# Linear attention and a squared-ReLU MLP in one kernel: the second half's two output products as one product by seven, with its sums made by accumulating transfers

## The chip, the cores and the metric

The kernel runs on one core of a Trainium2 chip. The metric is the device time of one execution in microseconds (us); the kernel before takes 407.9 us as the median of three runs (407.67 to 407.97). Durations and waits below come from one profiled execution of it, whose span is 406.3 us.

## The reference

```python
x = A_x                                   # 2048 tokens x 512 channels, float32
xn = layernorm(x)
# attention: 32 heads of 16 channels, no softmax
q, k, v = split(xn @ wqkv)                # phi(t) = t + 1 if t > 0 else exp(t); + 1e-6
kv = phi(k)^T v;  z = sum over tokens of phi(k)        # for each head
o = phi(q) @ kv / (phi(q) . z + 1e-6)
# MLP on x with 1376 hidden channels
h = relu(xn @ w1 + b1) ** 2
out = x + o @ wo + h @ w2 + b2
```

`xn` feeds both branches. `B_x` is not used.

## The kernel before, in words

All matrix products are float32 by three passes: an operand is split into a high part (the value rounded to the type that TensorE takes, a copy on ScalarE) and the rest (a subtraction on VectorE, `rest_of`, line 125, or the second half of `split`, line 122), and `PASSES` multiplies high by high, high by rest and rest by high. So each 128x128 by 128x512 product is three "wide" matmuls of 512 columns. A matmul of 256 columns is called a half here.

**The first quarter** (lines 526 to 1000) goes over 16 tiles of 128 tokens: normalise, transpose, project the keys, and sum `kx`. From it `matrix()` makes `m`, 512x512, which holds kv and `wo` in one, so that the attention output is `queries @ m`, where `queries` are phi(q) divided by the denominator.

**The main part** runs over two pairs of blocks of 512 tokens (`for n in range(2)`, line 1060): blocks 3 and 2, then blocks 1 and 0. In each pair:

- The loop over `p` (line 1194) makes the queries and the hidden units of both blocks: seven passes (`order`: two of queries, five of hidden units). A pass is a 2x2 block product made with seven products in place of eight (sums and differences of blocks ahead, sums of results behind). Each of the seven (`product`, line 494) is six wide matmuls. The operands on the weight side (`aop`) are made from w1 and wqkv with `chunk_sums`, `chunk_split` and `last_split`, in both pairs anew; those on the token side are `T`.
- Between these products stand the products of block t1's hidden units with w2 (`mlp_2`, line 502): a unit chunk of 128 takes 12 wide matmuls for a block of 512 tokens, into four accumulators.
- After the loop come the attention product of block t1, then for block t2 the same `mlp_2` for one chunk after the other, and its attention product. The last 96 hidden channels are apart: `last_2` and, for 32-row quarters, `quarters_2`.
- The attention product is `add_attention` in the first pair. In the second pair it is a product by seven again, for each block apart: class `Seven` (lines 1000 to 1054), whose matmuls are halves (`run`, line 1046), whose results are added to the residual by VectorE (`into`, line 1054).
- `steps_of` (line 421) turns each chunk of raw queries into divided ones: `phi_T`, `weighted`, `sums`, `quotients`, `divide`.

The residual x is loaded into `res`, the bias b2 is added to it by GpSimd's accumulating transfers (`add_bias`, line 1166, issued at line 1170), the accumulator is added by VectorE (`add`, line 1178), and the rows are stored (line 1182). The order of the work is written out by hand: `AT`, `AE` and `TM` (lines 1068 to 1086) say how many of the small steps go at which place. `matrix_sums` (line 975) prepares the sums of `m`'s blocks through DRAM. Every engine runs its instructions in program order; SyncE (SP) and GpSimd (POOL) issue transfers in program order too.

Of the kernel before, what the change touches and what calls it, by code (L numbers as in the profile page):

```python
# [13 lines left out]
P = 128  # L14
H = 32
# [3 lines left out]
def kernel(  # L19
# [400 lines left out]

    def steps_of(t, j, done=False, parts=False):
# [8 lines left out]
        def weighted():  # L430
            pz = w512(f"pz{t}_{j}", "p", 6)
            tiles.append(pz)
            nc.scalar.activation(pz, o, AF.Identity, bias=zc[:, 1, j:j + 1], scale=zc[:, 0, j:j + 1])  # L433

        def sums():
            pt = w512(f"pt{t}_{j}", "p", 6)
            den = small.tile([P, H], F32, name=f"dt{t}_{j}", tag="den")
            nc.vector.transpose(blocks(pt), blocks(tiles[0]))
            nc.vector.tensor_reduce(den, heads_of(pt), axis=AX.X, op=OP.add)
            tiles.append(den)  # L440

        def quotients():
            pz, den = tiles
            nc.vector.tensor_scalar(den, den, 1e-6, None, op0=OP.add)
            nc.vector.reciprocal(den, den)
            nc.vector.transpose(by_heads(heads_of(pz)), by_heads(den[:, :, None].to_broadcast([P, H, D // H])))

        def divide():
            nc.vector.scalar_tensor_tensor(o, o, 1e-6, tiles[0], op0=OP.add, op1=OP.mult)

# [524 lines left out]
    def matrix_sums(stage):  # L975

        t = [two(f"mr{r}") for r in range(2)]
        for r in range(2):
            nc.gpsimd.dma_start(t[r], md[:, 2 * r:2 * r + 2])
# [7 lines left out]
        def high(x, h, to, at):  # L987
            copy("act", h.bitcast(F32R), x)
            nc.gpsimd.dma_start(mtd[0][:, to, at], h)

        def low(x, h, to, at):
            nc.vector.tensor_tensor(out=x.bitcast(F32R), in0=x, in1=h, op=OP.subtract)
            nc.gpsimd.dma_start(mtd[1][:, to, at], x)
# [6 lines left out]
    class Seven:  # L1000

        def __init__(self, t, pairs=range(2)):
            self.t = t
            self.at = [slice(r * BT // 2 + pairs[0] * P, r * BT // 2 + (pairs[-1] + 1) * P) for r in range(2)]
            self.o = [[q[t][:, 2 * c:2 * c + 2, at] for c in range(2)] for at in self.at]

        def sums_o(self):

            (a11, a12), (a21, a22) = self.o
            return [lambda: self.op(a22, a21, a22, OP.add), lambda: self.op(a21, a11, a21, OP.subtract),  # L1010
                    lambda: self.op(a11, a22, a11, OP.subtract), lambda: self.op(a12, a12, a11, OP.subtract)]

        def op(self, o, x, y, how):
            nc.vector.tensor_tensor(out=o, in0=x, in1=y, op=how)

        def load_m(self):

            self.mt = both("mt", ("xs0h", "xs0l"))
            for o, src in zip(self.mt, mtd):
                nc.gpsimd.dma_start(f32(o), src)  # L1020

        def parts(self, src, to, order):

            highs, lows = [], []
            for c, at in order:
                h, l, x = (a[:, 2 * c:2 * c + 2, at] for a in (*to, src))
                highs.append(lambda h=h, x=x: copy("act", h, x))
                lows.append(lambda h=h, l=l, x=x: rest_of(l, x, h))
            return highs, lows

        def parts_o(self):

            self.s = both(f"so{self.t}", ("xs1h", "xs1l"))
            one, two = self.at
            return self.parts(q[self.t], self.s, ((1, one), (0, one), (0, two), (1, two)))

        def run(self, ps, left, right, e, first=False):

            c, r = left[1:]
            for i in range(2):  # L1040
                for n, (u, v) in enumerate(PASSES):
                    at = slice(r * (BT // 2) + e * P, r * (BT // 2) + (e + 1) * P)
                    a = aT[self.t, 2 * c + i][:, u, at] if left[0] == "a" else self.s[u][:, 2 * c + i, at]
                    w, k, z = right
                    b = (m if w == "m" else self.mt)[v][:, 2 * k + i, z]
                    nc.tensor.matmul(ps, lhsT=a, rhs=b, start=first and i == 0 and n == 0, stop=False,  # L1046
                                     skip_group_check=True)

        def into(self, ps, k, a):

            r = res[self.t, k][:, a]
            if a != LO and a != HI:
                r, ps = r.rearrange("p (a z) -> p a z", a=2), ps[:, None, :].to_broadcast([P, 2, D // 2])
            nc.vector.tensor_tensor(out=r, in0=ps, in1=r, op=OP.add)

    ALL = slice(0, D)

    last = TB - 1
    res = {}
    for n in range(2):  # L1060
        t1, t2 = NB - 1 - 2 * n, NB - 2 - 2 * n
        x1, x2 = xsb
        tag = "acc" if n else "ps"

        order = [("q", 0), ("w", 0), ("q", 1), *(("w", k) for k in range(1, NP))]
        NO = len(order)

        AT = (((0, 0, 0, 0, 0, 0, 0, 0, 0),
# [14 lines left out]
               (0, 0, 0, 0, 0, 0, 0, 2, 0)))[n]  # L1083
        AE = ((3, 1, 2, 3, 5, 2, 0, 1, 4, 5, 2),
              (2, 3, 2, 2, 0, 0, 0, 0, 0, 0, 0))[n]
        TM = {(1, 0): 4, (1, 4): 2, (1, 6): 1, (2, 4): 2, (3, 7): 1, (3, 0): 1, (4, 7): 1} if n else {}

        def matrix_step(p, at):
            do(m_sums, TM.get((p, at), 0))

        steps = {t1: [], t2: []}
        r2 = [work.tile([P, k, 512], F32, name=f"r2{u}{n}", tag=f"r{u}") for u, k in zip("abc", (4, 4, 3))]
        waiting = [*range(NF - 2, -1, -1), NF - 1]
        r2 = {f: r2[k // 4][:, k % 4] for k, f in enumerate(waiting)}
        m_sums = matrix_sums([r2[f] for f in waiting[:4]]) if n else []

        def last_units(rz):
            nc.scalar.activation(rz, rz, AF.Square)
            sz, rests = hidden_last(f"sz{n}", rz)

            def packed():
                lqs.append(quarters(f"sz{n}", rz, sz[0], work, "heads"))

            return sz, rests, packed

        lqs = []

        if n == 0:

            more()  # L1110
            pz2 = bank("pz0b")
            plain_1(pz2, z, x2)
            more()

            rz = r2[1]
            relu(rz, pz, NF - 1)
            relu(r2[NF - 1], pz2, NF - 1)
            do(extra, 2)
            values()
            do(extra, len(extra))  # L1120
        else:
            w2next = []
            pz = bank(f"pz{n}", "acc")
            plain_1(pz, z, x1)
        q.update({t1: four(f"q{t1}", "r2"), t2: four(f"q{t2}", "r1")})
        attention_places("r3", "r0")
        w = load_1(*order[1])
        s = {}
        if n:
            rz = w512(f"rz{n}", "p", 6)  # L1130
            relu(rz, pz, NF - 1)
            sz, sz_rests, packed = last_units(rz)
            sz_rests()
            packed()

        w2order = [NF - 1, *range(NF - 1)]

        def next_2(t):

            do(w2next, 2 - highs.pop(0))  # L1140
            if t + 1 < NF and (n == 0 or t >= TB - 1):
                f = w2order[t + 1]
                w2next.extend(piece_2(f, place(f)))

        def high_2():
            do(w2next)
            highs[0] = 1

        highs = [0] * NF
        if n:  # L1150
            next_2(0)


        banks = [bank(f"b{n}_{k}") for k in range(4)]
        t5, biased = None, []

        def load_res(t):
            for k in range(2):
                r = two(f"res{t}_{k}")
                i = t * TB + 2 * k  # L1160
                nc.sync.dma_start(r, xf[i * P:(i + 2) * P, :].rearrange("(i p) d -> p i d", i=2))
                for i in range(2):
                    res[t, 2 * k + i] = r[:, i, :]
                biased.append(r)

        def add_bias():
# [428 lines left out]
```

## Time and profile before

| | |
|---|---|
| median of three runs | 407.9 us |
| span of the profiled execution | 406.3 us |
| TensorE (PE) busy | 401.3 us, 99% |
| VectorE (DVE) busy | 329.2 us, 81% |
| ScalarE (ACT) busy | 273.3 us, 67% |
| GpSimd (POOL) busy | 57.3 us, 14% |
| moved by transfers | 55.31 MB, 136 GB/s over the span |
| GpSimd's transfer queue q0 | 9.44 MB |

How to read the profile: "PE" is the matmuls, "PEld" the loads of their stationary operand, which overlap them. In rows of a group, "x16 | 10.5, 688" is the count, the busy us in all and the mean ns of one. Matmuls are pipelined, so the time that one costs is read from the distance of starts and not from its 390 ns. In the table of stretches, "DMA share" is the mean busy share of the core's 16 transfer engines and GB/s what they moved. A few per cent of the matmul records are missing, so counts of matmuls are worked out from the code.

### The profile page before, as it was taken

The numbers are of one execution on the slowest core, as the hardware profiler recorded it, in microseconds if no ns is written. First come the engines' busy times: TensorE is split into PE (matmuls) and PEld (weight loads), VectorE is DVE, ScalarE is ACT, GpSimd is POOL, SyncE is SP. The second block draws the span as 40 slices with busy tenths as digits, with TensorE's granted clock in tenths as the row PEclk, the third lists the DMA queues.
The fourth block names the chain that finished last, engine by engine and source line by source line (L and its number), as shares of the span: only waits on it lengthen the run. The fifth ranks groups of instructions, "written<-read, shape, count | busy, mean of one in ns | idle before, by whom it ended". The sixth has DMA issues, their size and how long they took to land.

```text
span 406.3 us, 5887 instructions
## 1 busy us (share of the span) xinstructions
PE 401.3 (99%) x2011; PEld 334.1 (82%) x2011; DVE 329.2 (81%) x603; ACT 273.3 (67%) x478; POOL 57.3 (14%) x93
## 2 busy tenths in 40 slices
PE   8999999999999999999999999999999999999996
PEld 7888888888788888888878888888888888888895
DVE  5886666497898999988349998598989688989983
ACT  5777777456788789887728751578678857957430
POOL 5444333220000000030000300102200013000300
PEclk9999999999999999999999999999999999999999
DMA  5857656820463231291563912824331739306512
GB/s 210 275 166 230 208 157 205 241 45 0 121 193 80 77 103 27 85 224 29 186 231 124 227 38 91 231 53 129 122 113 52 207 110 305 53 34 224 105 26 105
DMA packets 48623, 55.31 MB, mean 136 GB/s; under 512 B 8593, under 2 KB 31377, under 8 KB 48082
## 3 DMA queue, kind: packets, MB, share of 16 engines
q1 hardware_dynamic: 44994, 45.50, 36.4%
q0 software_dynamic: 3520, 9.44, 9.9%
q8 instruction: 16, 0.26, 0.3%
q14 instruction: 13, 0.11, 0.1%
q10 hardware_dynamic: 80, 0.00, 0.0%
HBM read 40.90 MB, written 12.85 MB: 132 GB/s over the span
## 4 chain that ended last, share of the span: by engine, by line
PE 97%; DMA 1%; DVE 1%; ACT 0%; issue 0%
PE b L498 33%; PE acc L133 32%; PE pk L378 11%; PE kx L398 11%; PE acc L1046 2%; PE acc L509 2%; PE pz L133 1%; PE x L1046 1%; PE xl L1046 1%; DMA x<-in_A_x_dram 1%; PE b L133 1%; PE pz0b L133 1%; PE pt L310 0%; PE yl L1046 0%; PE y L1046 0%; PE acc L516 0%
## 5 line engine op out<-in xcount | busy, mean ns | idle before, releaser
L133 PE MATMUL acc<-w2r,s 128*128 128x512 f32 x477 | 113.0, 390 | 0.0
L133 PEld LDWEIGHTS acc<-w2r,s 128*128 128x128 f32 x477 | 89.3, 188 | 19.0 <-issue 0.7
L498 PE MATMUL b<-T,aop 128*128 128x512 f32 x336 | 83.5, 390 | 0.0
L498 PEld LDWEIGHTS b<-T,aop 128*128 128x128 f32 x336 | 63.0, 188 | 13.9 <-ACT t L114 0.8
L398 PE MATMUL kx<-pk,tok 128*128 128x512 f32 x192 | 46.0, 390 | 0.0
L398 PEld LDWEIGHTS kx<-pk,tok 128*128 128x128 f32 x192 | 36.0, 188 | 7.6 <-ACT pk L114 0.2
L1170 POOL DMA_DIRECT2D res<-in_B_b_dram x16 | 14.4, 1038 | 173.6 <-DVE S L736 85.9
L498 PE MATMUL b<-xs0h,aop 128*128 128x512 f32 x112 | 36.9, 391 | 0.0
L114 ACT ACTIVATE aop<-S 128x512 fp32r<-128x512 f32 x28 | 17.5, 624 | 13.1 <-DVE S L736 13.1
L359 POOL TENSOR_TENSOR tok<-xp,tok 128x512 fp32r<-128x512 f32 x15 | 19.8, 1320 | 39.8 <-ACT tok L114 39.8
L498 PEld LDWEIGHTS b<-xs0h,aop 128*128 128x128 f32 x112 | 21.0, 188 | 4.4
L125 DVE TENSOR_TENSOR w2r<-r,w2r 128x512 fp32r<-128x512 f32 (+2 forms) x35 | 23.8, 683 | 0.7 <-ACT w2r L114 0.6
L114 ACT ACTIVATE w2r<-r 128x512 fp32r<-128x512 f32 x32 | 19.6, 618 | 6.1 <-PE acc L133 4.7
L122 DVE TENSOR_TENSOR aop<-S,aop 128x512 fp32r<-128x512 f32 x28 | 19.3, 689 | 4.5 <-ACT aop L114 4.1
L498 PE MATMUL b<-xs0l,aop 128*128 128x512 f32 x56 | 21.8, 389 | 0.0
L122 DVE TENSOR_TENSOR s<-c,s 128x512 fp32r<-128x512 f32 x20 | 13.6, 689 | 7.6 <-ACT s L114 7.4
L498 PE MATMUL b<-xs1h,aop 128*128 128x512 f32 x56 | 19.5, 389 | 0.0
L114 ACT ACTIVATE T<-Tf 128x512 fp32r<-128x512 f32 x16 | 9.5, 625 | 14.4 <-DVE Tf L679 14.3
L114 ACT ACTIVATE c<-b 128x512 f32<-128x512 f32 x28 | 16.4, 585 | 2.8 <-PE b L498 2.6
L433 ACT ACTIVATE pz<-q,zc 128x512 f32<-128x512 f32 x16 | 12.9, 808 | 6.3 <-DVE q L419 6.3
L1178 DVE TENSOR_TENSOR res<-acc,res 128x512 f32<-128x512 f32 x16 | 10.5, 688 | 7.9 <-PE acc L133 5.1
L369 ACT ACTIVATE k<-pk 128x512 f32<-128x512 f32 x16 | 9.5, 593 | 9.7 <-PE pk L378 9.5
(265 smaller groups left out, 853.8 us busy)
## 6 DMA issues: line engine op xcount, KB each, us to landing
r<-in_B_w_dram SPq DMA_DIRECT2D x49, 256.0 KB, 3.5
res<-in_A_x_dram SPq DMA_DIRECT2D x8, 512.0 KB, 4.7
res<-in_B_b_dram POOLq DMA_DIRECT2D x16, 256.0 KB, 5.8
out_dram<-res SPq DMA_DIRECT2D x15, 256.0 KB, 2.1
via<-xp SPq DMA_DIRECT2D x5, 512.0 KB, 2.6
xg<-via SPq DMA_DIRECT2D x20, 128.0 KB, 2.8
xTd<-t SPq DMA_DIRECT2D x8, 256.0 KB, 3.4
x<-in_A_x_dram SPq DMA_DIRECT2D x4, 512.0 KB, 4.4
```

The costliest lines, as they stand in the source:

```text
L114: nc.scalar.activation(o, i, AF.Copy, bias=bias)
L122: ENG[el].tensor_tensor(out=l, in0=src, in1=f32(h), op=OP.subtract)
L125: nc.vector.tensor_tensor(out=l, in0=src, in1=f32(h), op=OP.subtract)
L133: nc.tensor.matmul(ps, lhsT=a[u], rhs=b[v], start=first and n == 0, stop=last and n == 2)
L359: ENG[el].tensor_tensor(out=l, in0=src, in1=f32(h), op=OP.subtract)
L378: nc.tensor.matmul(ps, lhsT=cols(i)[u][:, j, slot(i)], rhs=w[v][:, j, :], start=first and n == 0, stop=last and n == len(steps) - 1)
L398: nc.tensor.matmul(kxp[c], lhsT=tok[i][:, u, c * P:(c + 1) * P], rhs=pk[i][:, v], start=i == 0 and (u, v) == first, stop=i == NT - 1 and ( ...
L433: nc.scalar.activation(pz, o, AF.Identity, bias=zc[:, 1, j:j + 1], scale=zc[:, 0, j:j + 1])
L498: nc.tensor.matmul(ps, lhsT=a[u][:, j * P:(j + 1) * P], rhs=b[v][:, j, :], start=first and j == 0 and n == 0, stop=last and j == 1 and n == 2,
L1046: nc.tensor.matmul(ps, lhsT=a, rhs=b, start=first and i == 0 and n == 0, stop=False, skip_group_check=True)
L1170: nc.gpsimd.dma_start(r[:, i], b2[None, :].partition_broadcast(P), accum_op=OP.add)
L1178: nc.vector.tensor_tensor(out=r[:, a:z], in0=ps, in1=r[:, a:z], op=OP.add)
```

## The change

The first pair is as it was, but for two things: after each product its weight-side operand is stored to DRAM (`keep_operands`), and the differences of w2's blocks are made once (`w2_sums`: 12 subtractions on VectorE, stored to `w2sd`). The second pair is written anew:

- **Loop.** The seven passes run back to back without `mlp_2`. Operands come from DRAM (`load_operand`, 256 KB each, two passes ahead) in place of being split again. Sums of results go two ways: ScalarE copies one bank into another (with the bias) and the next product accumulates on it, or VectorE adds. Hidden units are kept squared, as float32, for both blocks: `h[r, c, k]` with r the block and c the parity of the chunk.
- **One product by seven** then does w2 and attention together: left is [hidden, queries] of both blocks (2x2: block by parity half), right is [w2; m] (2x2: parity half by output half). Each of the seven products, in the order M4, M1, M2, M6, M5, M7, M3, has parts 0, 1, 2 (five chunks of hidden units) and "q" (two chunks of queries): 42 wide matmuls, but for M3. M4 and M1 begin inside the loop's last pass.
- **Left sums** (`sum_of`) are four, made in place: sum 1 = A21 + A22, sum 3 = A21 - A11, sum 2 = sum 1 - A11, sum 4 = A12 - sum 2 up to sign, with A11 and A12 negated by ScalarE (`negate`). Each is four accumulating transfers from SBUF to SBUF on GpSimd's queue: three of 512 KB and one of 256 KB. M6 needs sum 2, M5 sum 1, M7 sum 3, M3 sum 4. Before its product a part is split (`left`): ScalarE's copy, VectorE's subtraction.
- **Output transposed.** For all but M3 the weights stand on the stationary side, every second column of 256 (`columns`), and 512 tokens stream; the result has channels on partitions. VectorE transposes it by 32x32 blocks (`turned_out`), and it is added to a residual block (`into`), by accumulating transfers of 256 KB or by VectorE. The residual blocks are loaded and stored in pieces of 32x16x64 (256 bytes in a row; `load_block`, `store_block`), 64 KB each. M3 is not transposed: 84 halves, added to rows that went out to DRAM and came back.

```diff
+    def keep_operands(p, *which):
+        for s in which:
+            nc.sync.dma_start(aopd[p][s], f32(src...))
+    def load_operand(p, name):
...
+        nc.sync.dma_start(f32(o), aopd[p][s][...])
...
-    class Seven:
...
-                nc.tensor.matmul(ps, lhsT=a, rhs=b, start=first and i == 0 and n == 0, stop=False,
...
+    def sum_of(n, *which):
+        for part in which:
+            o, a = (source(rc, part) for rc in SUMS_OF[n])
+            nc.gpsimd.dma_start(o, a, accum_op=OP.add)
+    def mul(name, ps, *which, first=False):
+        for part in which:
+            for a, b in zip(half_units[name, part], rights(name, part)):
+                for e in range(2):
+                    for n, (u, v) in enumerate(PASSES):
+                        nc.tensor.matmul(ps[e], lhsT=columns(b[u], e, None), rhs=a[v],
+    def turned_out(name, ps, half=None):
...
+                nc.vector.transpose(t.rearrange("p (b c e) -> p e b c", e=2, c=Q)[:, e],
+                                    by_blocks(src[e])[:, 8 * u:8 * u + 8])
+    def into(r, half, tiles, eng="dma"):
...
+                nc.gpsimd.dma_start(o, tiles[u], accum_op=OP.add)
...
+    sum_of(1, 1, 2)
+    mul("M4", X, 1, 2)
+    sum_of(3, 0, 1, 2)
+    load_block(0, 0, res_1[:, 0])
+    load_block(1, 1, res_1[:, 1])
+    left("M4", "q")
+    negate(0, "q")
+    sum_of(2, 0, 1, 2)
+    sum_of(1, "q")
...
+    sum_of(3, "q")
+    load_right("M5")
+    m1 = turned_out("M1", Ac, 0)
+    sum_of(2, "q")
+    m4 = turned_out("M4", X, 0)
+    into(0, 0, m1)
+    into(1, 0, m4)
+    mul("M2", Bc, 0, 1, 2, "q", first=True)
+    sum_of(4, 0, 1, 2, "q")
+    left("M6", 0, 1, 2)
+    load_right("M7")
+    mul("M6", Ac, 0, 1, 2)
+    left("M5", 0)
+    left("M6", "q")
+    mul("M6", Ac, "q")
...
+    into(0, 0, m2)
+    store_block(0, 0)
...
+    load_block(0, 1, res01)
+    mul("M5", Ac, 0, 1, 2, "q")
+    load_right("M3")
+    left("M7", 0, 1, 2, "q")
+    m5 = turned_out("M5", Ac, 1)
+    into(0, 1, m5, "dve")
+    store_block(0, 1, rowsd)
+    mul("M7", Y, 0, 1, 2, "q", first=True)
+    left("M3", 0, 1, 2, "q")
...
```

The denominator's 1e-6 moves into `zc`, which saves `steps_of` one small VectorE instruction for each chunk.

GpSimd's queue at its end, before: the sums of `m`'s blocks and the bias rows (`res`) of the second pair.

```order
L993 DMA mtld_1070<-mr0_2498 128x2x256
L993 DMA mtld_1070<-mr1_2499 128x2x256 x2
L1020 DMA mth_3238<-mthd_1069 128x2048
L1020 DMA mtl_3239<-mtld_1070 128x2048
L1170 DMA res1_0_3075<-in_B_b2_dram 128x512 x2
L1170 DMA res1_1_3077<-in_B_b2_dram 128x512 x2
L1170 DMA res0_0_3613<-in_B_b2_dram 128x512 x2
L1170 DMA res0_1_3615<-in_B_b2_dram 128x512 x2
```

The same place now, from the second part of sum 1 to the residual sum of M2. `h11`, `h10`, `h00`, `h01` are the hidden blocks, `h114` and `h4` their fifth chunks, `q0` and `q1` the queries, `res1` and `res10` residual blocks; L1596 is `sum_of`, L1719 `into`.

```order
L1596 DMA h10_2667<-h00_2665 128x1024 x2
L1596 DMA h4_2669<-h4_2669 128x512
L1596 DMA h00_2665<-h11_2668 128x1024 x2
L1596 DMA h4_2669<-h114_3098 128x512
L1596 DMA q0_2573<-q0_2573 128x1024
L1596 DMA q0_2573<-q1_2572 128x1024
L1596 DMA q1_2572<-q0_2573 128x1024
L1719 DMA res1_3341<-M1t0_3422 128x512
L1719 DMA res1_3341<-M1t1_3425 128x512
L1719 DMA res10_3093<-M4t0_3436 128x512
L1719 DMA res10_3093<-M4t1_3439 128x512
L1596 DMA h01_2666<-h00_2665 128x1024 x2
```

What moved: the bias transfers are gone (the bias is added by ScalarE in `turned_out`), the transfers of `m`'s sums went to SP, and in their place GpSimd issues all left sums, with the residual sums of M1 and M4 ahead of sum 4 and those of M2 behind it.

ScalarE at the M6 product, now (before, this stretch held the squares and splits of one unit chunk after the other). `M6_0` to `M6_q` are the parts of M6's left side, `rightM5` and `w2r0` M5's right side.

```order
L114 ACTIVATE M6_2_3508<-h4_2669 128x512
L114 ACTIVATE rightM5_3511<-T1r0_3412 128x2x256
L114 ACTIVATE rightM5_3511<-T1r2_3414 128x2x256
L114 ACTIVATE w2r0_1020<-T1r4_3416 128x256
L114 ACTIVATE M5_0_3554<-h11_2668 128x1024
L114 ACTIVATE M6_q_3557<-q1_2572 128x1024
L114 ACTIVATE M5_1_3572<-h11_2668 128x1024
```

What this shows: M6's last part stands behind M5's right side and first part on ScalarE; it reads `q1`, which is the last transfer of sum 2.

SP at the end, before: the last residual rows, and the last stores.

```order
L1161 DMA res0_0_3613<-in_A_x_dram 128x2x512
L1161 DMA res0_1_3615<-in_A_x_dram 128x2x512
L213 DMA w2r0_1020<-w2r0_1020 64x512
L478 DMA s1_0_10_3789<-s1_0_10_3789 64x512
L1182 DMA out_0_dram<-res0_0_3613 128x512 x2
L1182 DMA out_0_dram<-res0_1_3615 128x512
```

SP at the end now: `T3r` is M7's right side, `b22r` that of M3, `res01` the residual block that M5 and M3 end in, `rowsd` its way through DRAM.

```order
L1619 DMA T3r4_3522<-w2sd_1099 128x256
L1695 DMA out_0_dram<-res1_3341 32x16x64 x4
L1691 DMA res01_3615<-in_A_x_dram 32x16x64 x4
L1619 DMA b22r0_3669<-in_B_w2_dram 128x2x256
L1619 DMA b22r2_3671<-in_B_w2_dram 128x2x256
L1619 DMA b22r4_3673<-in_B_w2_dram 128x256
L1695 DMA rowsd_3699<-res01_3615 32x16x64 x4
L1941 DMA rows_3767<-rowsd_3699 128x4x256
```

What moved: a store of finished output, which waits for M2's residual sum, now stands ahead of the last residual block and of the last operand loads; before, no operand load stood behind a store there.

More of the change, by code (lines that the diff above doesn't have):

```diff
@@ L978, in matrix_sums @@
         for r in range(2):
-            nc.gpsimd.dma_start(t[r], md[:, 2 * r:2 * r + 2])
+            nc.sync.dma_start(t[r], md[:, 2 * r:2 * r + 2])
         def op(o, x, y):
@@ L998, in matrix_sums @@
                                                               (low, 1), (low, 2), (low, 3)))]
-    class Seven:
[L1002 to L1054, printed above, removed]
@@ L1554 @@
[L1554 to L1566 removed]
+                next_2(fa + 1)
@@ new lines @@
+            product(C, S1, [T[1][:, u] for u in range(2)], True)
+            keep_operands(p, 2)
+            t5_ = w512(f"t5_{p}", "p", 6)
+            copy("act", t5_, C)
+            step(at_p[1])
+        else:
+            do(bias, 2)
+            mlp_2(acc, pa, s.pop(pa))
+        if was:
+            product(before, A22b, [T[4][:, u] for u in range(2)], False, True)
+            if was == "w":
+                c21 = w512(f"c21_{p}", "p", 6)
+                relu(c21, before, pb)
+            elif p == 1:
+                copy("dve", q[t1][:, pb], before)
+            else:
+                phi_T(q[t1][:, pb], before)
+                steps[t1] += steps_of(t1, pb, True, True)
@@ new lines, with second_sums @@
+        if kind == "w":
+            high_2()
+        if p == 0:
+            last_sums(4, difference_high, difference_low)
+        if kind == "w":
+            relu(r2[fa], c12, fa)
+        else:
+            steps[t2] += steps_of(t2, fa)
+        step(at_p[5])
+        if kind == "w" and fa:
+            next_2(fa + 2)
+        def second_sums(f=pb, first=not was):
+            if first:
+                for k in range(TB):
+                    last_2(acc[k], k, sz, True, False)
+            else:
+                mlp_2(acc, f, s.pop(f))
@@ new lines @@
+    for k in range(TB):
+        at = slice((2 + k % 2) * Q, (3 + k % 2) * Q)
+        nc.tensor.matmul(ends[k], lhsT=zq[0][at, k * P:(k + 1) * P], rhs=w2s["q"][at, HI], start=False, stop=False)
+    chunks = [(a, b) for part in (0, 1, 2, "q") for a, b in zip(half_units["M3", part], rights("M3", part))]
+    for k in range(TB):
+        for n, (a, b) in enumerate(chunks):
+            three(ends[k], [v[:, k * P:(k + 1) * P] for v in a], b, False, n == len(chunks) - 1)
+        nc.vector.tensor_tensor(out=rows[:, k], in0=ends[k], in1=rows[:, k], op=OP.add)
+        i = t1 * TB + k
+        nc.scalar.dma_start(of[i * P:(i + 1) * P, HI], rows[:, k])
```

1149 lines of the change are left out of this document (706 added, 443 removed), and 21 rows, old and new, of the table AT.

## The prediction

> **What bounds the kernel now.** First the page's busy times and slices:
>
> ```profile
> span 406.3 us, 5887 instructions
> PE 401.3 (99%) x2011; PEld 334.1 (82%) x2011; DVE 329.2 (81%) x603; ACT 273.3 (67%) x478; POOL 57.3 (14%) x93
> ...
> PE   8999999999999999999999999999999999999996
> PEclk9999999999999999999999999999999999999999
> DMA  5857656820463231291563912824331739306512
> ```
>
> TensorE is full in every slice between the first and the last, at full clock; the transfer engines are busy in bursts. The chain of waits says the same:
>
> ```profile
> PE 97%; DMA 1%; DVE 1%; ACT 0%; issue 0%
> ```
>
> So matmuls set the time, and I need the price of each kind. TensorE's timeline gives it, as the distance of starts:
>
> ```profile
> 363.23 22.04 PE L133 MATMUL acc<-w2r,s 128*128 128x512 f32 x96
> 385.10 0.28 PE L1046 MATMUL xl<-mh,aTsr 128*128 128x256 f32 x1
> ...
> 395.13 3.59 PE L133 MATMUL acc<-w2r,s 128*128 128x512 f32 x15
> ...
> 402.24 0.40 PE L509 MATMUL end<-w2r,s 128*128 128x256 f32 x2
> ```
>
> A wide matmul costs (385.10 - 363.23) / 96 = 0.228 us. Between 385.10 and 395.13 stand the 84 halves of one block's attention product: 10.03 / 84 = 0.119 us each, slightly over half a wide one. The last matmul starts at 402.24, 4.1 us before the end.
>
> What could become late is read from the table of stretches (columns: span, busy us and counts of PE, PEld, DVE, ACT, POOL, clock, DMA share, GB/s): the halves, the loop, the first pair's second part, the loop of the second pair.
>
> ```profile
> 385.10:395.10 10.00, 10.00 (x85) 10.00 (x84) 8.54 (x16) 4.55 (x9) 0.00 (x0) 1.00 0.12 26
> 120.00:160.00 40.00, 40.00 (x178) 33.14 (x177) 36.87 (x70) 33.52 (x60) 0.00 (x0) 1.00 0.28 77
> 200.00:240.00 40.00, 40.00 (x182) 32.60 (x182) 32.13 (x56) 26.07 (x44) 3.56 (x4) 1.00 0.63 187
> 280.00:320.00 40.00, 40.00 (x179) 33.12 (x178) 36.02 (x69) 31.25 (x58) 4.04 (x6) 1.00 0.41 122
> ```
>
> VectorE works up to 36.9 us of 40 and TensorE still doesn't wait; transfers have room.
>
> **Matmuls.** By the code, the second pair's w2 and attention take 251 wide matmuls, 178 halves and 8 quarters before. Now: six products of 42 wide are 252, with 12 for the last channels 264; M3's 84 halves and 8 more, and some ten small pieces. That is 13 x 0.228 = 3.0 us more and 86 x 0.119 = 10.3 us less: **-7.3 us**, and 400.6 us in place of 407.9 if nothing waits.
>
> **First pair.** Storing operands (28 of 256 KB) goes where the DMA share was 0.28. Making w2's differences adds 12 subtractions to VectorE:
>
> ```profile
> L122 DVE TENSOR_TENSOR aop<-S,aop 128x512 fp32r<-128x512 f32 x28 | 19.3, 689 | 4.5 <-ACT aop L114 4.1
> ```
>
> 12 x 0.69 = 8.3 us, beside the first pair's attention (48 wide, 10.9 us) and w2 products. In 200 to 240, VectorE has 7.9 us free. I take 0; without that cover it is the 8.3.
>
> **The loop without `mlp_2`.** Each pass is 42 wide matmuls, 9.57 us. The attention steps that lay beside twice the matmuls now stand close together:
>
> ```profile
> L446 DVE STREAM_TRANSPOSE pz<-dt 128x512 f32<-128x512 f32 x16 | 11.4, 712 | 0.6
> L438 DVE STREAM_TRANSPOSE pt<-pz 128x512 f32<-128x512 f32 x16 | 11.3, 704 | 0.0
> L439 DVE TENSOR_REDUCE dt<-pt 128x32 f32<-128x512 f32 x16 | 11.0, 686 | 0.6
> L445 DVE RECIPROCAL dt<-dt 128x32 f32<-128x32 f32 x16 | 5.7, 353 | 0.6
> ```
>
> With two 0.69 operations, one step costs VectorE 3.8 us; eight cost 31. Adds and squares of five unit passes, four each at 0.69, are 14; the adds of the two query passes 5.5; left parts of M4 and M1 8.7; right sides 3.5: about 63 of 67 us. In the windows above VectorE kept 92% with TensorE full; 94% is at the edge. Token-side sums lie ahead of the loop as before. I take 0, up to 3 as an upper end; a gain is excluded, as TensorE was full. Dropped splits of aop free VectorE and ScalarE only.
>
> **Weights by every second column.** No row loads weights with a step. Contiguous ones:
>
> ```profile
> L498 PEld LDWEIGHTS b<-T,aop 128*128 128x128 f32 x336 | 63.0, 188 | 13.9 <-ACT t L114 0.8
> ```
>
> 188 ns lie under the 228 of a wide matmul. Up to 228 ns a stepped load costs nothing; doubled (376) it would cost 0.15 x 252 = 37 us. I take 0, since there is no row to say that the step costs.
>
> **The accumulating transfers.** This decides. After's sums are 16 transfers (12 of 512 KB, 4 of 256 KB: 7.3 MB), the residual sums by transfer 12 of 256 KB (3.1 MB): 10.5 MB, nearly all within the last 80 us. The only accumulating transfers of before are the bias, four at a time:
>
> ```profile
> 175.76 2.90 POOL L1170 DMA_DIRECT2D res<-in_B_b_dram  x3 [85.94 <-DVE S L736]
> 180.58 0.89 POOL L1170 DMA_DIRECT2D res<-in_B_b_dram  x1 [1.91 <-issue]
> ```
>
> and all of them by their line:
>
> ```profile
> L1170 POOL DMA_DIRECT2D res<-in_B_b_dram x16: 853/990/1295, 175.8 to 381.1; - x16
> ...
> DMA to landing us min/median/max: 4.5/5.8/10.3
> ```
>
> GpSimd takes 1 us to issue one, and holds the fourth back. What the wires did meanwhile, beside plain loads elsewhere:
>
> ```profile
> 178.00:184.00 6.00, 6.00 (x28) 4.95 (x28) 4.75 (x9) 5.26 (x9) 1.56 (x2) 1.00 0.96 153
> 339.00:342.00 3.00, 3.00 (x15) 2.47 (x14) 1.99 (x4) 2.94 (x6) 0.85 (x1) 1.00 1.01 327
> 69.00:70.00 1.00, 1.00 (x6) 0.82 (x5) 0.71 (x3) 0.97 (x3) 0.00 (x0) 1.00 0.90 365
> ```
>
> With all 16 engines busy (0.96), accumulating moved 153 GB/s where plain transfers move 327: a byte accumulated costs the engines two. For rows of 4 KB, as the sums have, the bound is half of 365 / 0.90, 203 GB/s; I take 180 for sums, 153 for residual sums: 7.3 / 0.18 + 3.1 / 0.153 = 61 us of all 16 engines. The plain transfers of that stage (m's parts 2.1 MB, right sides 3.3, residual blocks and stores 4.7) are some 10 MB at 327: 31 us. Together 92 us, in a stage whose matmuls take 76. The Trainium skill says under "DMA: Bandwidth & Descriptors", "Issuing engines are not separate DMA queues", that transfers from all issuers run on the same 16 engines and interleave. That speaks against the change; the share of 0.96 agrees.
>
> Now the chain to TensorE, with T = 0 at M4's first matmul. In program order at 0.228 and 0.119 the matmuls would reach M6's "q" part at T = 41.8, end M7 at 64.8, start M3 at 65.9, end it at 75.9.
>
> - Sum 1 waits for the squares of `h11` in the last pass, T = 6.9. The landing minimum of 4.5 for 256 KB, less 1.6 to 1.7 of data, leaves 2.9 fixed: 9.8. Until sum 2's "q" about 5 MB remain, at 180 GB/s 27.7: T = 37.5. Twice one "q" sum waits for another's landing with nothing left queued, 2 x 2.9: 43.3. Plain transfers beside it take about 3 (0 to 8): 46.3. ScalarE's copy and VectorE's rest:
>
> ```profile
> L114 ACT ACTIVATE xs1h<-xT 128x1024 fp32r<-128x1024 f32 x2 | 2.0, 1044 | 0.0
> L125 DVE TENSOR_TENSOR xs1l<-xT,xs1h 128x1024 fp32r<-128x1024 f32 x2 | 2.4, 1221 | 0.0
> ```
>
> +2.3 gives T = 48.6 against 41.8: **a wait of 6.8 us** at M6's "q" part (3 to 14).
>
> - M3: after sum 2, the residual sums of M1 and M4 (1.05 MB, 6.9), sum 4 (1.8 MB, 10.2) and those of M2 (0.5 MB, 3.4) end at T = 66.8. SP's next instruction is a store that needs M2's sum, and behind it stand the last residual block and M3's right side. Eleven issues and a landing, by one load line's row (0.38 us each)
>
> ```profile
> L186 SPq DMA_DIRECT2D r<-in_B_w_dram x26: 367/379/807, 73.3 to 314.5; - x26
> ```
>
> and, of the list of transfers, the median from issue to landing:
>
> ```profile
> r<-in_B_w_dram SPq DMA_DIRECT2D x49, 256.0 KB, 3.5
> ```
>
> 11 x 0.4 + 3.5 = 7.9: T = 74.7. M3's right copy and rest take 2.4, the left parts' rests on VectorE behind it 4.4: T = 81.5 to 82.2 for the last part, and three chunks of 21 halves, 7.5, remain: M3 ends at T = 89.7 in place of 75.9. That holds the first wait too: **+13.8 in all** (+3 to +18). The end behind it stays 4 us.
>
> GpSimd's waits block only its own transfers, and those are the chain above. Bias transfers and aop splits that go had cover before, so nothing is gained by them.
>
> The Trainium skill ("TensorE: Matmul & The Clock Gate", Part 1) has the clock fall after TensorE idles for some us. That would add to each wait; no row here shows it, as TensorE never idles.
>
> **Rivals.**
>
> *The sums fit (faster).* If an SBUF-to-SBUF accumulate costs what a plain copy does, 10.5 MB take 32 us instead of 61, T = 46.3 becomes 30, before 41.8, and sum 4 lands in time. Then 400.6 plus small gaps: 401 to 406. The point is a wait of 7.3 us in all. For: the bias came from DRAM, from one row for all partitions, which may be the slow part of it. Against: all 16 engines were busy (0.96) while they moved half the bytes, which is what two reads for each write would look like. The Trainium skill's fit in "DMA: Bandwidth & Descriptors", "Anatomy of one DMA — SWDGE (gpsimd) path" (2.0 us + bytes / 436 GB/s) would give 24 us for these bytes, an estimate; the window with 153 GB/s disagrees.
>
> *The loop overflows as well (slower).* VectorE's 63 us in 67 are late by up to 3 us from the fourth pass on, ahead of the first sum, so that the whole chain moves with it, beside the upper end of the transfers' range: 417 to 426. It decides once VectorE's load passes TensorE's 67.
>
> *Stepped weights cost (slower).* 400.6 + 37 = 438 and more; for: in the halves' window PEld was full, so loads do bound TensorE there; against: nothing.
>
> *No difference.* Waits of 6.5 to 8.1 us just cancel the gain: 407.1 to 408.7.
>
> *It doesn't do what it says*: if halves were not limited by their loads, 84 of them would cost 9.57 rather than 10.03; the saving shrinks by 0.4 us. Too small to decide.
>
> **How the numbers follow.** The profiled execution takes 406.3 in its span; the median is 407.9, 1.6 more, which I keep. 407.9 - 7.3 + 13.8 = **414.4 us**. Chances: waits at M6 and M3 by queued accumulates, 409 to 418: 0.48; sums fit, faster: 0.30; overflow as well: 0.13; stepped weights 0.04; no difference 0.05. 0.2% (0.8 us) is about what a measurement of this kernel can tell from no change. Faster 0.30, same 0.05, slower 0.65. The range leaves out the stepped weights, the far end of the overflow, and a few in a hundred below 402: 402 to 424. The slower cases by themselves span 409 to 424.
>
> **What would show it.** In the profile after: TensorE with two gaps, ended by ScalarE's or VectorE's part of M6 "q" (some 7 us, behind a transfer of `q1`) and by M3's right or left side (some 7 more); slices of DMA at 9 through the last 70 us; GpSimd's issue row with landings over 5 us; wide matmuls at 0.228. Wrong if the landings of 512 KB sums come within 3 to 4 us of issue with the DMA share well under 0.9 (the sums fit), if stepped weights show PEld over 228 ns, or if TensorE waits inside the loop for VectorE.

## The result, and the profile after

The changed kernel takes 430.99 us (median of four runs, 428.74 to 432.77) against 407.94: a ratio of 1.0559, with a 95% interval of 1.0525 to 1.0594. The forecast was 414, with 402 to 424. The sign was right and the size was wrong: 23 us slower where 6.5 were forecast. The span of its profiled execution is 431.0 us, that of before 406.3, and the 24.7 us between them are accounted for below. The profiled execution is the longest of the four (432.77 us), so that this sum lies 1.8 us above the median.

The page of the changed kernel, the same rows as before (busy tenths of 40 slices of 10.8 us, and the granted clock):

```profile
span 431.0 us, 5854 instructions
...
PE   8999999999799999999999999999999999399657
...
PEclk9999999999899999999999999999999999879959
DMA  6856656602987764898969848978999999799956
```

TensorE was full before. Now it has holes in three places, slice 10 (some 110 us), slice 34 (370) and slices 37 to 39 (405 on), and at each of them the clock falls too. The transfer engines stand at 9 through most of the last third. The waits of TensorE name the holes (columns: who waited, for whom, us in all, times, longest):

```profile
PE end L133 <- ACT M L1554: 8.4, 1, 8.4
PE a L1658 <- ACT M_q L114: 6.9, 1, 6.9
PE b L522 <- ACT c L114: 3.2, 2, 3.0
...
PE a L1658 <- DVE M_q L122: 0.5, 1, 0.5
PE end L133 <- DVE M L1555: 0.5, 1, 0.5
```

The first two are the two gaps of the forecast: M3's left side (8.4, then 0.5 for VectorE's rest of it) and M6's "q" part (6.9 and 0.5). The third was not in it, and lies in the first pair. ScalarE's timeline there, and the issues of SP that belong to it, in order of time:

```profile
104.95 0.50 SPq L1036 DMA_DIRECT2D aop_0d<-aop  x1
...
112.33 0.63 ACT L114 ACTIVATE aop<-r 128x512 fp32r<-128x512 f32 x1 [3.42 <-DMA aop_0d<-aop]
112.86 0.58 ACT L114 ACTIVATE c<-b 128x512 f32<-128x512 f32 x1
...
113.49 2.76 PE L522 MATMUL b<-T,aop 128*128 128x512 f32 x6 [2.98 <-ACT c L114]
```

The first pass's operand is stored from 104.95 on, by the new `keep_operands`. The next pass's operand goes into the same tile, so ScalarE waits 3.42 us until the store has read it; the copy of a bank stands behind on ScalarE, and TensorE behind that.

What the transfer engines did in the last stage, by queue (packets, MB, share of 16 engines; from 318 us to the end):

```profile
q0 software_dynamic: 4032, 10.49, 51.4%
q1 hardware_dynamic: 21143, 10.70, 39.9%
```

Over those 113 us the accumulating transfers held all 16 engines for 58 us (181 GB/s) and the plain ones for 45 us (237 GB/s). The table of stretches shows the clock around the wait at M6 (last three columns: clock, DMA share, GB/s):

```profile
369.00:371.00 2.00, 0.77 (x4) 0.30 (x2) 0.03 (x1) 0.00 (x0) 0.19 (x1) 1.00 0.03 6
371.00:373.00 2.00, 0.00 (x0) 0.00 (x0) 0.00 (x0) 0.00 (x0) 2.00 (x3) 1.00 0.48 92
373.00:375.00 2.00, 0.00 (x0) 0.00 (x0) 0.00 (x0) 0.00 (x0) 0.45 (x1) 0.53 0.95 172
...
381.00:383.00 2.00, 2.00 (x6) 1.56 (x5) 0.45 (x1) 0.00 (x0) 0.88 (x1) 0.50 1.05 195
383.00:385.00 2.00, 2.00 (x8) 1.23 (x8) 1.11 (x3) 0.00 (x0) 0.57 (x1) 0.91 1.04 195
```

TensorE stops at 369.8; the clock is halved from about 373 on. Matmuls start again at 376.6, and the clock stays at half to 383.4, so the first twelve run at 0.43 us each and not at 0.23. Behind M3's wait it is the same, from about 411 to 421. The two restarts, and the four matmuls behind M6's "q" part:

```profile
376.64 0.80 PE L1658 MATMUL a<-M_q,mth 128*128 128x512 f32 x1 [6.87 <-ACT M_q L114]
...
382.76 1.37 PE L1666 MATMUL x<-sz,w2r 128*128 128x512 f32 x4
...
414.13 0.80 PE L133 MATMUL end<-rightM,M 128*128 128x256 f32 x2 [8.39 <-ACT M L1554]
```

The first row of the table shows something else: at 369 to 371, and by finer windows to 372, the transfer engines move almost nothing (0.03). The sum of queries that M6 needs waits there for the landing of the one ahead of it, with nothing queued, as the forecast had it. So the engines are full over most of this stage, but M6's wait is in part this chain.

The sum, in spans. The second pair starts 5.4 us late (256.69 in place of 251.28): 2.8 by the first pair's wait, 1.7 by the half clock behind it (113.7 to 117.1), 0.9 by small losses further on. The second pair has 11 wide matmuls more and 82 of 256 columns less (the small pieces of 32 rows counted in), -7.3 as forecast. Its waits are 16.2 (8.4 + 0.5 + 6.9 + 0.5, by the timeline). The half clock behind them costs 3.1 at M6 (6.12 us for twelve matmuls that take 2.8, less the 0.47 of the wait inside, and 0.3 on the four behind them) and 3.1 at M3 (13.6 for what takes 10.0, less 0.46). What is left of the pair's 171.1 us (151.4 before), 4.7, is a slower pace; this term is a remainder and not a row. The end behind the last matmul is 0.5 shorter. 5.4 - 7.3 + 16.2 + 6.2 + 4.7 - 0.5 = 24.7.

### The profile page after: what moved, and what is told of

It is laid out like the page before. It is cut to its first block, busy times and chain, and to the rows that moved or that the text cites. A ratio compares the mean times of both kernels' runs of the same rounds, so it can differ in the third digit from the quotient of the medians.

```text
span 431.0 us, 5854 instructions
## 1 busy us (share of the span) xinstructions
PE 406.6 (94%) x1940; PEld 332.3 (77%) x1940; DVE 314.4 (73%) x539; ACT 265.6 (62%) x444; POOL 67.0 (16%) x101
## 4 chain that ended last, share of the span: by engine, by line
PE 77%; DMA 9%; ACT 4%; DVE 3%; issue 3%; SPq 2%; POOL 0%; ACTq 0%; DVEq 0%; POOLq 0%
PE b L522 18%; PE acc L133 17%; PE pk L378 10%; PE kx L398 10%; PE b_c L522 4%; PE b_a L522 4%; PE a L1658 3%; PE end L133 3%; DMA T1r<-w2sd 3%; PE b_b L522 2%; DMA aop_0d<-aop 2%; SPq L1691 1%; DMA b22r<-in_B_w_dram 1%; PE x L1658 1%; PE pz L133 1%
## 5 line engine op out<-in xcount | busy, mean ns | idle before, releaser
L133 PE MATMUL acc<-w2r,s 128*128 128x512 f32 x240 | 57.0, 390 | 0.0
L133 PEld LDWEIGHTS acc<-w2r,s 128*128 128x128 f32 x240 | 44.9, 188 | 9.9 <-issue 0.4
L522 PE MATMUL b<-T,aop 128*128 128x512 f32 x168 | 43.2, 400 | 3.2 <-ACT c L114 3.2
L522 PEld LDWEIGHTS b<-T,aop 128*128 128x128 f32 x168 | 31.8, 191 | 11.6 <-ACT c L114 4.1
L1596 POOL DMA_DIRECT2D h<-h x12 | 10.4, 866 | 110.8 <-PE b_b L522 89.5
L122 DVE TENSOR_TENSOR M<-h,M 128x512 fp32r<-128x512 f32 (+1 forms) x17 | 15.5, 940 | 6.2 <-ACT M L114 6.0
L522 PE MATMUL b<-xs0h,aop 128*128 128x512 f32 x56 | 18.9, 398 | 0.0
L114 ACT ACTIVATE M<-h 128x512 fp32r<-128x512 f32 (+1 forms) x17 | 13.4, 822 | 7.1 <-PE b_a L522 3.3
L133 PE MATMUL acc<-mh,aTsr 128*128 128x512 f32 x48 | 15.6, 390 | 0.0
L386 DVE SCALAR_TENSOR_TENSOR pk<-k,pk 128x512 fp32r<-128x512 f32 x16 | 11.3, 708 | 4.1 <-ACT pk L114 3.4
```

Of the source, the lines that this page charges most:

```text
L114: nc.scalar.activation(o, i, AF.Copy, bias=bias)
L122: ENG[el].tensor_tensor(out=l, in0=src, in1=f32(h), op=OP.subtract)
L133: nc.tensor.matmul(ps, lhsT=a[u], rhs=b[v], start=first and n == 0, stop=last and n == 2)
L386: nc.vector.scalar_tensor_tensor(pk[i][:, 1], p, 1e-6, f32(pk[i][:, 0]), op0=OP.add, op1=OP.subtract)
L522: nc.tensor.matmul(ps, lhsT=a[u][:, j * P:(j + 1) * P], rhs=b[v][:, j, :], start=first and j == 0 and n == 0, stop=last and j == 1 and n == 2,
L1596: nc.gpsimd.dma_start(o, a, accum_op=OP.add)
```

## The experiments

**The first operand stored early.** If the wait in the first pair is for the landing of that one store, issuing it earlier removes it.

```diff
+    keep_operands(0, 0)                    # right behind the last preparations
     ...
-            keep_operands(p, 0, 3)
+            keep_operands(p, *((0, 3) if p else (3,)))
```

> Edit: the store of the first pass's first operand (512 KB) is issued as soon as the operand is made, ahead of the two loads of w1 on SP; the small bias load moves behind. Theory A (in the first pass ScalarE's next copy into that operand waits for the store to land, TensorE stands for 3.0 us and then runs at half clock for some us, 5.7 us lost in all): the wait falls to under 1 us, the start of the first attention product moves from 241.2 to about 236 us, the time from 431.0 to about 425.5. Rival B (the transfer engines are simply full there, so that the order does not help): the store still lands as late, TensorE's wait stays at 2 to 4 us and the time at 429 to 432.

Measured: 429.45 us, ratio to before 1.0526 (1.0491 to 1.0561). The wait went and the first attention product starts at 236.5, as theory A has it; the time hardly moved. The waits in its profile tell why:

```profile
PE end L133 <- ACT M L1555: 11.7, 1, 11.7
PE a L1659 <- ACT M_q L114: 6.8, 1, 6.8
```

The second pair started 4.7 us earlier (252.01), and M3 waited 3.3 us longer: it started at 411.4 in place of 414.1. The end was set by what M3 waits for and not by what TensorE had behind it.

**Matmuls that nobody reads, in the two gaps.**

```diff
+    keep_warm(X[0], 30)
     mul("M6", Ac, "q")
     ...
+    keep_warm(bank_0, 34)
     for k in range(TB):
         last_2(ends[k], k, zs[0], True, False, D // 2, D)
```

> Edit: 30 matmuls whose results nobody reads stand ahead of M6's q part, 34 ahead of M3, each group a little shorter than the wait measured there. Theory A (after each wait the clock is granted at half for several us, 2.8 us lost behind the first and 3.1 behind the second): the granted clock stays at 1.00 in both places, M6's q part starts as late as before but takes 2.8 us and not 6.1, M3 takes 10.5 us and not 13.6: about 425. Rival B (the slow matmuls behind the wait are slow because of their operands, which have only just been written): the pace there stays at 0.43 us and the time at 431 or a little more.

Measured: 427.75 us, ratio 1.0501 (1.0469 to 1.0534). The page's clock row:

```profile
PEclk9999999999999999999999999999999999999999
```

Twelve matmuls of M6's "q" part now take 3.5 us and not 6.1, with operands as fresh as before. So the slow pace behind the waits is the clock. Of M3's 3.1 us only 1.4 came back (12.2 us from its first matmul in place of 13.6): at full clock it outruns the splits of its left side and waits for them three times (0.8, 0.2 and 0.4 us), behind a first wait of 1.0. That is why the time stayed above the 425 of theory A. The first pair's wait was 2.3 us in this execution and no half clock followed it, which no edit caused: 3.0 us of its span's gain are that.

**Sums as plain copies** (the sums are left out).

```diff
-            nc.gpsimd.dma_start(o, a, accum_op=OP.add)
+            nc.gpsimd.dma_start(o, a)
```

> Edit: the sixteen transfers of the left sums copy instead of adding (the sums are left out, so the output is another). Same bytes, same order, same waits. Theory A (an accumulated byte costs the 16 engines two plain ones, 7.3 MB at about 180 GB/s, and the stage is limited by its transfers): the queue of accumulates shrinks by some 20 us of all engines, M6's q part waits for under 2 us, M3 for under 5, and the time falls to 412 to 420. Rival B (the chain of landings sets the waits, each sum waiting for the one ahead of it): the landings stay at 5 us and more, the waits at 5 us and more, and the time at 426 or more.

Measured: 416.57 us, ratio 1.0225 (1.0208 to 1.0242), 14.4 us below the changed kernel. M6's wait is gone, M3's is 2.7. The same 10.49 MB on GpSimd's queue, in the same window from 318 to 412 us, the changed kernel first:

```profile
q0 software_dynamic: 4032, 10.49, 61.8%
```

and with copies:

```profile
q0 software_dynamic: 3776, 10.49, 42.8%
```

58 us of all engines become 40, and 18 us less for the 7.3 MB of sums is close to what "one accumulated byte costs two" gives (41 us against half of it). Theory A holds for the waits and the time. Of rival B one sign came true: a 512 KB transfer still took 5.2 to 5.4 us to land (7.3 and 6.1 before), but with that the chain was in time.

**Adjacent weight columns.**

```diff
-        return at.rearrange("p (c e) -> p e c", e=2)[:, e]
+        return at.rearrange("p (e c) -> p e c", e=2)[:, e]
```

> Edit: the stationary operands of the transposed products take 128 adjacent columns in place of every second one of 256 (the output's channels come out in another order). Theory A (the step costs the load of the weights a little, so that a wide matmul there takes 0.233 to 0.238 us and not 0.228): the pace in M2, M5 and M7 falls to 0.228, and the time by 1 to 2 us where no wait takes it up, to 429 to 431. Rival B (the pace is that of the transfers' writes into SBUF, or of where the tiles lie): it stays at 0.233 to 0.238.

Measured: 430.26 us, ratio 1.0548 (1.0524 to 1.0573), not to be told from the changed kernel's. But the loads of weights show it. With a step, in the changed kernel (behind the bar: busy us in all, mean ns):

```profile
L1658 PEld LDWEIGHTS a<-M,w2r 128*128 128x128 f32 x24 | 4.6, 193 | 1.0
```

and with adjacent columns:

```profile
L1658 PEld LDWEIGHTS a<-M,w2r 128*128 128x128 f32 x24 | 4.5, 188 | 1.0
```

M2, M5 and M7, 126 matmuls, take 29.6 us with the step and 28.95 without; M7 alone goes from 0.2333 to 0.2267 us a matmul. The step costs 5 ns a load, some 1.3 us over the 252 matmuls; a rival of 37 us was far off.

**The last loads ahead of the store.**

```diff
     load_right("M7")
+    load_right("M3")
     ...
     into(0, 0, m2)
+    load_block(0, 1, res01)
     store_block(0, 0)
```

> Edit: on SP, M3's right side (three loads) and the last residual block (four pieces) stand ahead of the store that waits for M2's residual sum. Theory A (M3 waits because SP's order holds its loads behind that store, and because the pieces with 256-byte rows take 1.1 to 1.7 us each to issue): M3's wait of 8.4 us goes, and with it the half clock behind it, 11 to 12 us, M6's wait stays at 7: 419 to 421. Rival B (the 16 transfer engines are full from 318 to 411 us, so what is moved ahead pushes the sums back): M6's wait grows or M3 still waits, and no more than half is gained: 425 to 430.

Measured: 422.63 us, ratio 1.0364 (1.0335 to 1.0393), between the two theories. M3 doesn't wait at all any more, and M6 still does (6.2). M3's first matmuls in the profile:

```profile
402.06 1.70 PE L133 MATMUL end<-rightM,M 128*128 128x256 f32 x12
```

They start at 402.1 and not at 414.1, so SP's order was what held M3 last; 2.6 of those 12 us are a shorter wait in the first pair in this execution.

**Four sums of sixteen on VectorE.**

```diff
+            if part == "q":
+                nc.vector.tensor_tensor(out=o, in0=a, in1=o, op=OP.add)
+            else:
                 nc.gpsimd.dma_start(o, a, accum_op=OP.add)
```

> Edit: the four sums of queries (512 KB each, of the sixteen sums) are made by VectorE, 1.2 us each, and not by accumulating transfers. Theory A (full transfer engines, an accumulated byte costing two): 2.1 MB less accumulating frees 11 to 12 us of all engines; M6's wait goes with its half clock, and M3 starts earlier by some 10 us: 410 to 421. Rival B (only the chain of three landings ahead of M6's q part is late): M6's wait and half clock go, but M3's loads come when they came before, M3 still starts near 414: 426 to 430.

Measured: 415.46 us, ratio 1.0168 (1.0134 to 1.0202). M6's wait is gone, and M3 starts 16 us earlier:

```profile
398.09 0.80 PE L133 MATMUL end<-rightM,M 128*128 128x256 f32 x2 [4.29 <-ACT M L1554]
```

Of the 16, the wait at M6 and its half clock are 10 and the first pair 1.4; M3 still waits 4.3, with half clock behind it. M3's loads had not been moved: they came earlier because the residual sum that their store waits for did (the store is issued at 378.2 and not at 393.8). That is theory A.

**All sums on VectorE**, and then the three edits together.

```diff
-            nc.gpsimd.dma_start(o, a, accum_op=OP.add)
+            nc.vector.tensor_tensor(out=o, in0=a, in1=o, op=OP.add)
```

> Edit: all sixteen left sums on VectorE (12 of 1.2 us, 4 of 0.7: 17 us more work there), no accumulating transfers but the residual sums. Theory A (full transfer engines): some 40 us of all engines go, both waits shrink to under 2 us each, and what stays is the first pair's loss of 5.7 us and the slower pace: 408 to 414. Rival B (VectorE, with the sums ahead of M4's q part and M2's right side in its order, becomes the bound from there on): TensorE waits for VectorE in M4's q part or M2, 3 to 8 us with half clock behind it: 415 to 424.

> Edit: the three together: left sums on VectorE, the first operand stored early, the last loads ahead of the store. Theory A: each takes away its own loss; 5 us below the version with the sums on VectorE alone, 403 to 408, level with the kernel before or faster by up to 1%. Rival B (VectorE's order is the bound): waits for VectorE stay, 410 to 418.

Measured: 416.70 us, ratio 1.0215 (1.0174 to 1.0256), and 412.93 us, ratio 1.0118 (1.0097 to 1.0138). Both are in rival B's range. Neither waits for a transfer in the last stage; both wait for VectorE, but at M6's first part and not at M4 or M2. TensorE and VectorE of the three edits together:

```profile
358.04 2.31 DVE L1597 TENSOR_TENSOR h<-h,h 128x1024 f32<-128x1024 f32 x2
360.28 0.68 DVE L1597 TENSOR_TENSOR h<-h 128x512 f32<-128x512 f32 x1
360.88 1.21 DVE L1597 TENSOR_TENSOR q<-q 128x1024 f32<-128x1024 f32 x1
362.02 2.95 DVE L122 TENSOR_TENSOR M<-h,M 128x1024 fp32r<-128x1024 f32 x3
...
363.28 4.93 PE L1659 MATMUL a<-M,rightM 128*128 128x512 f32 x20 [2.81 <-DVE M L122]
```

The 4 us of sum 4, which only M3 needs, stand ahead of the rests that M6 waits for.

**Sum 4 by transfers again, or later on VectorE** (each with the other two edits).

```diff
+            if n == 4:
+                nc.gpsimd.dma_start(o, a, accum_op=OP.add)
+            else:
                 nc.vector.tensor_tensor(out=o, in0=a, in1=o, op=OP.add)
```

> Edit: the version with all three changes, but sum 4 (2.1 MB with its queries) goes by accumulating transfers again. Theory A (VectorE's 4.0 us of sum 4 stand ahead of the rests of M6's first part, which makes TensorE's last wait of 2.8 us; the transfer engines have room there now): the wait goes and nothing comes in its place, 409 to 411. Rival B (those transfers fill the engines again just where M7's right side and M3's loads are due): M7 or M3 waits 2 us or more, 412 to 416.

Measured: 408.58 us (ten runs), ratio 1.0030 (1.0018 to 1.0043): the best version, 1 us slower than the kernel before. Theory A, and a little under its 409; nothing came in the place of the 2.8 us. (Sum 4 is 1.8 MB with its queries, three transfers of 512 KB and one of 256.) Its page:

```profile
span 406.4 us, 5837 instructions
...
PE   7999999999999999999999999999999999999996
PEclk9999999999999999999999999999999999999999
DMA  6857646910898846789696974896798846499987
```

```diff
     m2 = turned_out("M2", Bc)
+    sum_of(4, 0, 1, 2, "q")
```

> Edit: the version with all three changes, all sums on VectorE, but sum 4 stands behind M5's left parts and M2's turned output in VectorE's order. Theory A (only the order on VectorE made the last wait): the 2.8 us go, 409 to 411, like the version with sum 4 by transfers. Rival B (VectorE is full there in any order): the wait moves to M5's or M7's left side, 412 to 415.

Measured: 414.04 us, ratio 1.0160 (1.0137 to 1.0184). The time is in rival B's range, but neither theory had the place. M6's left side came in time, but now sum 4 stood ahead of the transposes that empty M6's banks, and M5 writes into the same banks:

```profile
374.42 8.42 PE L1659 MATMUL a<-M,rightM 128*128 128x512 f32 x24 [3.79 <-DVE M6t L1711]
```

24 matmuls at 8.42 in place of 5.6 us are the half clock behind a wait of 3.8.

**Long rows for the residual loads** (elements of x land elsewhere).

```diff
-            nc.sync.dma_start(res_rows(o, g), token_rows(r, half, g, xf))
+            nc.sync.dma_start(o[Q * g:Q * (g + 1)]..., xf[t:t + 64, :]...)
```

> Edit: the changed kernel as it was, but the 16 pieces of the residual blocks are loaded with rows of 4 KB in place of 256 bytes, the same bytes from the same range of x (elements land elsewhere, so the output is another). Theory A (short rows cost the engines and the issue: plain transfers in this stage reach 237 GB/s and not 327, and a piece takes 1.2 us to issue): a piece issues in about 0.4 us, M3's loads come 4 to 6 us earlier, M3's wait of 8.4 us shrinks by that: 424 to 427. Rival B (the bytes and the accumulates alone fill the engines): no change beyond 1 us, 429.5 to 431.5.

Measured: 428.65 us, ratio 1.0519 (1.0486 to 1.0551); M3's wait went from 8.4 to 8.0, so most of the 2.3 us lies elsewhere (the second pair started 1.3 earlier). The plain queue's share of the window fell from 39.9% to 33.8%, so short rows do hold the engines longer. Over all 16 pieces, 128 KB each by the list of transfers (not 64), the median issue fell from 1.24 to 0.83 us. But the issue of the last four, which stand ahead of M3's loads, takes nearly as long as before, the changed kernel first:

```profile
398.43 6.61 SPq L1691 DMA_DIRECT2D res<-in_A_x_dram  x4
...
396.35 6.10 SPq L1692 DMA_DIRECT2D res<-in_A_x_dram  x4
```

1.65 us each with rows of 256 bytes, 1.5 with rows of 4 KB. At 316 us, where less is queued, four such pieces take 2.08 and 1.84 us in all, 0.5 each. That SP waits here to hand over to a full queue fits this, and is not shown.

## Why the prediction was wrong

**Matmuls, -7.3: right.** The best version, without a wait of note, shows that it is there; it is spent elsewhere.

**The accumulating transfers: right, at M3 by luck in part.** All 16 engines for 61 us was the estimate, 58 the measurement, and the copies showed that the adding is about half of it. M6's "q" part was to wait 6.8 us and waited 6.9, and 0.5 for the rest, and the chain ahead of M3 was right to 1 us: the store that needs M2's sum is issued at 393.8, 67.8 us behind M4's first matmul (325.97), where 66.8 was forecast. M3 was to wait another 7.0 and waited 8.9, but here two errors cancel. From that store to the landing of M3's first load I had 7.9 us, eleven issues at 0.4 and a landing of 3.5; it took 16.5 (to 410.3). And TensorE came to M3 7 us later than forecast, mostly by the half clock and the pace. The plain transfers were put at 31 us and took 45: I used the rate of long loads for pieces with short rows; with rows of 4 KB they took 37.

**The clock: the step that failed first, 6.2 us.** I left the half clock out of the sum, because no row of before showed it, and named it in a sentence only. It costs 3.1 us behind each of these two waits, and 1.7 more in the first pair. The Trainium skill ("TensorE: Matmul & The Clock Gate", Part 1) puts it at an idle window of about 3.4 us, free-running against the program. The trace agrees: at M6 the clock fell 3.4 us after the last matmul, at M3 some 5. The free running shows too: with all sums on VectorE a wait of 2.81 us was followed by half clock, and with the three edits the same wait, 2.81 us, was not. A forecast of a wait of 7 us should have carried 2 to 3 us behind it.

**Storing operands, taken as 0: the second that failed, 5.4 us with the half clock behind it.** I weighed the stores by the DMA share of the windows, 0.28, and put their number at 28 of 256 KB; 21 of them are 512 KB. Neither is the cause: a store reads a tile that is written again one pass later, so it adds a wait to the writer; in the first pass, which has no `mlp_2` between its products, 7.4 us from issue to landing were too many. "Work the stores hide behind" was the wrong question; "who writes this tile next, and when" was the right one. Issuing that store earlier gave back 4.7 of the 5.4.

**The pace, taken as 0: about 4.7 us.** I had it that a stepped load under 228 ns costs nothing, and the step in the weights is 1.3 of the 4.7. In the loop, products whose operands lie in the tiles `A` and `S` take 0.233 us, and those in `slot` 0.227 to 0.232, with weight loads of 188 ns in both; the 300 wide matmuls ahead of M4 take 69.3 us where 0.227 makes 68. The rest is not resolved to rows. Why these tiles are slower is open; no run here tried it. M3's 84 matmuls of 256 columns did not get slower: 0.119 us each at full clock.

**VectorE in the loop, taken as 0 to 3: 0.** No wait for it shows between 260 and 325 us.

**The rivals.** The faster one, "the sums fit", is excluded by the share of q0. The slower one named VectorE in the loop, which was not it. My range ended at 424, because it took each cost once: what stood behind a cost (the clock behind a wait, a write behind a store) was in none of its ends. With those two, 414.4 + 6.2 + 5.4 = 426.0, and the pace makes it 430.7; the waits were 2.4 longer than forecast and the end 0.5 shorter, which makes 432.6, and the profiled execution took 432.77.

**Where the gain goes at best.** In the version without waits the second pair takes 149.8 us (252.73 to 402.49) where its matmuls at the old pace make 144.1, and starts 1.45 late: of 7.3 us, 5.7 go to pace and small waits and 1.45 to the first pair, and the rest is within what two profiled executions differ by.

## What to carry to other kernels

A transfer that adds costs the 16 engines about twice its bytes, so a sum of 512 KB that VectorE makes in 1.2 us held all engines for some 2.9; moving arithmetic to transfers pays only where the engines have that time free, and here they were taken for nearly all of 318 to 412 us (61.8% and 37.0% by the two queues). Price a long wait on TensorE with half clock behind it: each wait of 3.8 us or more in these profiles was followed by it, at a loss of 1.7 to 3.1 us; of the waits of 1.8 to 3.0 us some were, at 1.3 to 1.7, and some were not. Look for the next writer of each tile that a new store reads. In a queue that runs in order, what is needed last must not stand ahead of what is needed next: a store ahead of loads cost some 8 us here, and sum 4 ahead of a rest or of a transpose 3 to 4.

## What the runs showed of the hardware that I had not expected

- A matmul's stationary operand with every second column takes 193 ns to load and not 188, and the pace follows by the same 5 ns, though the load lies under the matmul before it.
- The half clock comes in steps of 3.4 us. By windows of 0.2 us it lasts from 113.7 to 117.1, 373.1 to 383.4 and 410.7 to 420.9 in the changed kernel, 3.4, 10.2 and 10.2 us, and every stretch of it in the other profiles that ends inside the run is 3.4, 6.8, 10.2 or 13.7. So the loss is not set by the wait alone: behind M6's waits of 6.9 us here and 6.8 in the version with the first operand stored early, it lasts 6.7 and 3.8 us from the first matmul on.
- Handing a transfer of 128 KB over took SP 1.5 to 1.65 us each at 396 to 405 us and 0.5 at 316, with rows of 4 KB as with rows of 256 bytes; over all 16, longer rows made it shorter in the median (0.83 and 1.24).
- Taking 4.7 us out of the first pair gained 1.5 us in the median (430.99 to 429.45) and 2.6 in the span: M3, whose loads stand behind a chain of transfers, waited 3.3 longer.
